# Transformer block on one core: rows dealt 16 to a partition, and gate/up weights loaded by column groups in one ring

## The chip, the cores and the metric

The kernel runs on one core of one Trainium2 chip. Its time is device microseconds of that core, from launch to end. A profile of one execution goes with it: TensorE (PE, and its weight loads PEld), VectorE (DVE), ScalarE (ACT), GpSimd (POOL), SyncE (SP) and the 16 DMA engines.

## The reference

The input x has 2048 tokens (rows) of 448 features, in bf16. Part A is a linear attention block with 16 heads of 28, part B a gated MLP of width 1792. Every step works on one row alone except the two sums over all tokens (kv and z).

```python
n = layernorm(x)
q, k, v = split(n @ wqkv)                      # 16 heads of 28
pq, pk = phi(q), phi(k)                        # phi(t) = (t + 1 if t > 0 else exp(t)) + 1e-6
kv = sum over tokens of pk (x) v ;  z = sum over tokens of pk
o = (pq @ kv) / (pq . z + 1e-6)
h = x + o @ wo
m = layernorm(h)
out = h + (gelu_tanh(m @ w_gate) * (m @ w_up)) @ w_down
```

## The kernel before, in words

The 2048 rows are 16 tiles of 128. `xv` and `outv` (the views of x and the output in DRAM) deal row t*128 + p to partition p of tile t. All x stays in `x_sb`, and the results are written into it before they go out.

*Order of the work.* The kernel is a list of numbered tasks with their buffers. For each engine the string `ORDERS` gives the order in which its queue holds them; semaphores carry the dependences between engines. An engine never overtakes: what stands behind a waiting instruction waits too. The task numbers shift when a task is added, so the strings of two versions can't be compared number by number. SP's queue issues nearly all DMAs, ACT's queue a few.

*Stage 1, attention sums.* For each tile, DVE takes layer-norm statistics (L347, L348), ACT makes the reciprocal deviation (L354, L356), DVE (tiles 0 to 3, L369) or POOL (the others, L351 and L387) normalizes into `xnn`, a ring of six tiles. The normalized tile is transposed into `xnT`: tiles 0 to 3 on PE (L377) with evictions on ACT and DVE, the others by a DMA transpose that SP issues (L389). Then the K projection (L403 with `wk_sb`, 4 matmuls), its feature map on ACT and DVE (L414 to L416), and `pt`, the sum over tokens of normalized x times pk (L422, 4 matmuls, accumulated over all tiles in four PSUM banks). Q projections (L403 with `wq_sb`) are put between them and behind them.

*Stage 2, turn to outputs.* After the last `pt`, its sums are evicted, kv is made with `wv_sb` (L459), masked on DVE (L463), multiplied with `wo_sb` (L468) and evicted to `w2` (L471, L473). For each pair of tiles, function `a2_pair`: the query features (L480, L481), their products with z (`t1`, L485, nearly all on POOL), a reduction to the denominators `den` (L488), the added epsilon (L490), the reciprocal (L491), and the scaled features `pqn` (L492). These are transposed to `pqnT`: pair 0 on PE (L501), the others by DMA (L507). PE multiplies with `w2` (L520), DVE adds x (L526), and a second layer norm gives `hn` (L538, L555), which is transposed to `hnT` (tiles 0 and 1 on PE at L547, the others by DMA at L558).

*Stage 3, MLP.* In chunks of 2, 2, 4, 4 and 4 tiles, `gu_chunk` multiplies with gate and up. The 448 features lie in seven pieces of 64: gate's weights occupy partitions 0 to 63 of `wgu_sb`, up's partitions 64 to 127, and a gate matmul (L600) runs beside an up matmul (L602). ACT applies gelu (L620), DVE multiplies (L622), `b2_tile` does the down projection (L572), the last add (L576) and the store (L577). The work of later pairs is interleaved with the chunks.

*Loads.* Helper `dma` (its issue is L281) keeps the loads of one queue in order. `dma_w3` loads the first 384 rows of a weight, `dma_w1` the last 64, which wait for POOL's zero fill of their padding (L299). SP's queue before: x tile 0, wk, x 2–3, wq, x 4–5, x 6–7, x 8–11, x 12–15, wv, three token transposes, wv's tail, nine token transposes, wo, gate, then pair 1's `pqnT` transpose, w_down, and so on. ACT's queue: x tile 1, the tails of wk and wq, and, behind the landing of the last token transpose, up. Gate and up are one DMA each, 1568 KB.

Of the kernel before, what the change touches and what calls it, by code (L numbers as in the profile page):

```python
# [6 lines left out]
F32 = mybir.dt.float32  # L7
# [7 lines left out]
ORDERS = (  # L15
    "29 35 37 66 46 44 76 71 62 64 53 55 79 92 82 70 87 75 131 86 102 114 91 126 106 141 118 153 130 165 145 177"
    " 157 169 194 189 204 181 216 228 193 243 208 220 232 247 248 233 258 252 287 249 289 293 291 255 264 295 311"
    " 261 313 315 267 316 276 270 273 352 329 333 430 435 440 445 450 455 383 460 502 414 465 507 512 517 522 527"
    " 468 532 574 579 584 486 537 589 594 599 604 609 614 619 624 629 634 639 558 540 671 647 702 644 653 718 723"
    " 728 733 650 738 743 748 753 758 763 768 773 778 783 800 805 810 815 820 825 830 835 840 845 850 855 860 865"  # L20
    " 788 791 794 797 870 873 876 879 882",
    "4 6 9 28 32 33 41 36 42 59 60 45 50 51 67 78 77 54 97 72 98 109 63 93 110 83 80 121 122 94 88 136 81 137 148"
    " 149 133 160 132 103 172 115 173 161 127 142 184 211 199 223 185 212 200 224 154 238 166 239 178 195 190 205"
    " 196 217 229 244 280 281 284 234 285 260 254 253 259 235 250 290 251 294 256 266 312 257 314 263 265 269 268"
    " 262 323 277 324 272 325 326 271 278 275 330 274 335 433 431 438 436 443 441 448 446 453 451 456 458 461 463"
    " 503 505 508 510 515 513 518 520 525 523 528 530 535 533 575 577 582 580 585 587 590 592 597 595 600 602 605"
    " 607 612 610 615 617 620 622 625 627 630 632 640 635 637 642 721 719 726 724 731 734 736 729 741 739 744 746"
    " 751 749 756 754 759 761 766 764 769 771 774 776 781 779 786 784 801 803 806 808 811 813 816 818 823 821 826"
    " 828 833 831 838 836 841 843 848 846 851 853 858 856 863 861 868 866",
    "30 31 39 34 40 57 38 58 43 48 61 49 47 107 52 95 65 96 68 56 108 69 73 119 74 134 120 146 135 84 158 85 159"  # L30
    " 147 89 170 90 171 221 182 104 105 116 197 117 338 198 128 209 222 210 183 129 236 143 299 144 237 155 297 156"
    " 167 168 179 298 180 191 300 336 192 206 368 207 218 219 230 339 231 337 369 245 246 283 282 301 286 303 370"
    " 307 304 308 305 309 288 342 306 343 346 292 310 347 401 344 296 348 345 349 317 399 318 371 319 320 374 321"
    " 327 322 375 328 378 331 376 332 402 353 334 356 400 354 357 355 358 377 434 432 379 409 380 439 437 410 405"
    " 381 444 442 687 471 411 363 449 406 447 543 689 545 473 407 366 408 472 412 452 454 459 546 457 387 384 388"
    " 474 389 690 544 477 385 386 504 464 418 481 462 415 419 506 420 416 417 394 478 482 397 509 511 553 656 483"
    " 516 554 514 425 519 658 521 428 466 657 659 479 484 480 526 531 524 549 688 529 555 536 534 666 576 550 578"
    " 556 581 662 583 588 551 490 552 667 469 491 487 586 591 593 663 664 598 596 488 489 601 603 668 693 492 606"
    " 608 613 694 611 616 500 618 695 621 623 697 626 628 669 698 631 633 699 497 665 696 641 700 538 636 559 562"
    " 563 541 564 560 561 643 672 675 676 569 648 673 677 572 674 706 638 703 645 704 722 720 705 727 682 725 732"  # L40
    " 707 708 654 730 737 735 716 713 742 740 745 747 752 750 757 755 760 762 685 767 765 770 772 775 777 651 782"
    " 780 787 785 802 804 807 809 812 814 817 819 824 822 827 829 834 832 839 837 842 844 849 847 852 854 859 857"
    " 862 867 864 789 792 869 795 798 871 874 877 880 883",
    "17 0 1 18 19 20 22 21 23 26 24 99 111 100 27 112 2 123 124 138 162 150 139 174 151 163 175 186 213 225 201 187"
    " 240 202 25 214 226 241 302 340 341 372 373 404 403 360 359 361 365 362 475 476 547 391 390 392 393 396 548 421"
    " 422 423 424 427 660 661 692 691 493 494 495 496 499 566 565 567 568 571 679 678 680 681 684 710 711 709 715"
    " 712",
    "3 5 7 8 10 11 12 13 14 101 113 125 15 140 152 164 176 188 203 215 227 242 16 279 350 351 382 364 367 413 395"
    " 398 426 467 429 485 557 470 498 670 501 701 539 542 573 570 655 717 646 683 714 649 686 652 790 796 793 799"
    " 875 872 881 878 884",  # L50
)
# [119 lines left out]
def bass_sequential_preLN__linear_attn_block__glu_gated_geglu__prompt_kernel(  # L171
# [4 lines left out]
    NG, GW = 4, 112  # L176
    NK = 7
    NJ = FF // 128
    EPS_LN, EPS = 1e-5, 1e-6
# [9 lines left out]
    with es:  # L189
        block = es.enter_context(nc.Block())  # L190

        def sb(name, shape, dt):
            return es.enter_context(nc.sbuf_tensor(name, shape, dt))
# [36 lines left out]
        t1 = sb("t1", [128, 2, D], F32)  # L230
        den = sb("den", [128, 4, H], F32)
        rd = sb("rd", [128, 4, H], F32)
# [17 lines left out]
        b_wk, b_wq, b_wv = bufs("wk", 2), bufs("wq", 2), bufs("wv", 2)  # L250
        b_wo, b_wg, b_wu, b_wd = _Buf("wo"), _Buf("wg"), _Buf("wu"), _Buf("wd")
        b_ident, b_ones, b_mones, b_mtmp, b_mask, b_eps, b_mhalf, b_powtmp = (
# [21 lines left out]

        xv = A_x[0].rearrange("(t p) d -> p t d", p=128)
        outv = out[0].rearrange("(t p) d -> p t d", p=128)

# [7 lines left out]
        def op(eng, fn, r, w, name, after=()):  # L285
            return G.add(eng, fn, r=r, w=w, name=name, after=after)

        def dma_w3(q, dst, c0, b, name):
            return dma(q, dst[:, 0:3, :], A_wqkv[0:384, c0:c0 + D].rearrange("(k p) n -> p k n", p=128), [b[0]], name)

        def dma_w1(q, dst, c0, b, name):
            return dma(q, dst[A_, 3, :], A_wqkv[384:448, c0:c0 + D], [b[1]], name)


        def dma_x(q, a, b):
            dma(q, x_sb[:, a:b, :], xv[:, a:b, :], b_x[a:b], "dx%d" % a)
# [5 lines left out]
        dma_w3("sp", wk_sb, D, b_wk, "dwk")  # L302
        tk = dma_w1("act", wk_sb, D, b_wk, "dwk_t")
        dma_x("sp", 2, 4)
        dma_w3("sp", wq_sb, 0, b_wq, "dwq")
        dma_w1("act", wq_sb, 0, b_wq, "dwq_t")
        dma_x("sp", 4, 6)
        dma_x("sp", 6, 8)
        dma_x("sp", 8, 12)
        dma_x("sp", 12, 16)  # L310
        dma_w3("sp", wv_sb, 2 * D, b_wv, "dwv")
        dma_w1("sp", wv_sb, 2 * D, b_wv, "dwv_t")
        dma("sp", wo_sb[:, :, :], A_wo.rearrange("(g p) n -> p g n", p=GW), [b_wo], "dwo")

# [49 lines left out]
        def ln_tile(t):  # L364
# [20 lines left out]
            else:  # L385
                ln_negm(t, t + 1, mv1, nm1, b_mv1, b_nm1, "1")
                op("pool", lambda e: e.tensor_scalar(xnn[:, i, 0:D], x_sb[:, t, :], nm1[:, t:t + 1], rs1[:, t:t + 1], ALU.add, ALU.mult),  # L387
                   [b_x[t], b_nm1[t], b_rs1[t]], [b_xn[i]], "normP_%d" % t)
                G.add("sp", lambda e: e.dma_start_transpose(xnT[:, t, :, :], xnn[:, i, :]), r=[b_xn[i], b_ones2], w=b_xnT[t], name="xT_%d" % t, kind="dma")  # L389

# [50 lines left out]
        xts = [t for t in G.all if t.name.startswith("xT_")]  # L441
        dma("sp", wgu_sb[A_, :, :], B_w_gate.rearrange("(k p) n -> p k n", p=64), [b_wg], "dwg", after=xts[-1:])
        dma("act", wgu_sb[B_, :, :], B_w_up.rearrange("(k p) n -> p k n", p=64), [b_wu], "dwu", r=b_xnT[T - 1])

# [31 lines left out]
        def a2_pair(p):  # L476
# [9 lines left out]
            for t in (a, a + 1):  # L486
                n, i = t % 2, t % 4
                op("dve", lambda e, n=n, i=i: e.tensor_reduce(den[:, i, :], t1[:, n, :].rearrange("p (h d) -> p h d", h=H), AX.X, ALU.add),  # L488
                   [b_t1[n]], [b_den[i]], "dr_%d" % t)
                op("dve", lambda e, i=i: e.tensor_scalar(den[:, i, :], den[:, i, :], EPS, None, ALU.add), [b_den[i]], [b_den[i]], "de_%d" % t)  # L490
                op("dve", lambda e, i=i: e.reciprocal(rd[:, i, :], den[:, i, :]), [b_den[i]], [b_rd[i]], "rd_%d" % t)  # L491
                op("dve", lambda e, t=t, n=n, i=i, i2=i2: e.tensor_tensor(  # L492
                    pqn[:, i2, n, :, 0:GW].rearrange("p g (h d) -> p g h d", h=4), pq[:, t, :].rearrange("p (g h d) -> p g h d", g=NG, h=4),
                    rd[:, i, :].rearrange("p (g h) -> p g h", g=NG).unsqueeze(3).to_broadcast([128, NG, 4, DH]), ALU.mult),
                   [b_pq[t], b_rd[i]], [b_pqn[i2][n]], "pn_%d" % t)
# [85 lines left out]
        def gu_chunk(t0, nt):  # L581
# [4 lines left out]
            for j0 in range(0, NJ, nj):  # L586
# [5 lines left out]
                def fngu(e, W, j0=j0, psG=psG, psU=psU):  # L592
# [10 lines left out]
                    return ins  # L603
                G.add("pe", fngu, r=[b_hnT[t % HR] for t in tiles] + [b_wg, (b_wu, 1)], w=[(b_ps[BK_G[i]], 0), (b_ps[BK_U[i]], 1)], name="gu%d_%d" % (nt, v), mw=True)
                for hh_ in range(2):
# [82 lines left out]
```

## Time and profile before

| | us |
|---|---|
| median of 5 runs | 200.31 (198.77 to 202.58) |
| profiled execution, own time | 202.58 |
| its span, first to last instruction | 200.8 |
| PE busy | 191.4 (95%), 1572 matmuls |
| DVE busy | 133.2 (66%) |
| ACT busy | 74.4 (37%) |
| POOL busy | 50.4 (25%) |
| mean granted TensorE clock | 0.983 |
| gate load, issue to landing | 14.6 |
| up load, issue to landing | 17.1 |

The profile cuts the span into 40 slices of 5 us; a digit is the busy share of an engine in a slice in tenths (9 is 90% or more), and PEclk is the clock that the TensorE was granted, in tenths. In the timeline, a line gives the start, the duration, the engine, the source line, the operation, what it writes and reads, and in brackets how long the engine was idle before it and what the profile holds responsible; "SPq" and "ACTq" are DMA issues. Ends of matmuls are modelled, so distances between starts tell PE's pace better than durations. The profiled execution is the slowest of the five runs.

### The profile page before, as it was taken

How to read it: one execution, taken by the hardware profiler on the slowest of the kernel's cores; microseconds unless marked ns; L12 is line 12 of the kernel's file. 1: busy time of each engine (PE TensorE's matmuls, PEld its weight loads, DVE VectorE, ACT ScalarE, POOL GpSimd, SP SyncE). 2: the span in 40 equal slices, each digit the busy share in tenths (PEclk: the TensorE clock that was granted, in tenths of full speed). 3: DMA queues.
4: the chain of work that ended last, by engine and by line, in shares of the span. 5: the costliest groups of instructions: out<-in, count | busy, mean ns of one | idle time of the engine just before them, and what ended most of it. 6: DMA issues, size and time to landing. Idle time of an engine off the chain costs nothing.

```text
span 200.8 us, 4146 instructions
## 1 busy us (share of the span) xinstructions
PE 191.4 (95%) x1572; PEld 109.7 (55%) x1572; DVE 133.2 (66%) x371; ACT 74.4 (37%) x210; POOL 50.4 (25%) x92
## 2 busy tenths in 40 slices
PE   7899999988699989999999999999999999999993
PEld 7454455544478657854444355544455667745563
DVE  2899859899478988968686889536455554433221
ACT  3796543888533221413043220022334434410000
POOL 6074640632270278144004005505000000000000
PEclk9999999999759999999999999999999999999999
DMA  5945448999902912570300092400802000000211
GB/s 171 361 114 83 92 86 207 210 217 137 344 3 42 134 25 45 121 98 0 75 3 0 12 172 64 91 0 26 175 23 56 0 0 3 0 11 16 69 46 49
DMA packets 36180, 16.98 MB, mean 85 GB/s; under 512 B 27712, under 2 KB 35264, under 8 KB 36160
## 3 DMA queue, kind: packets, MB, share of 16 engines
q1 hardware_dynamic: 35392, 14.88, 34.9%
q10 hardware_dynamic: 768, 1.84, 4.3%
q8 instruction: 12, 0.20, 0.4%
q14 instruction: 8, 0.07, 0.1%
HBM read 8.26 MB, written 1.84 MB: 50 GB/s over the span
## 4 chain that ended last, share of the span: by engine, by line
PE 74%; DVE 15%; DMA 6%; SPq 1%; issue 1%; ACT 0%; POOL 0%; ACTq 0%; DVEq 0%
PE ps L600 28%; PE ps L572 21%; PE ps L602 11%; PE ps L520 5%; PE ps L403 4%; PE ps L422 4%; DVE st L347 2%; DMA hnT<-hn 2%; DMA x_sb<-in_A_x_dram 2%; DVE den L488 2%; DMA xnT<-xnn 1%; DVE pqn L492 1%; DVE hh L622 1%; DVE den L490 1%; SPq L281 1%
## 5 line engine op out<-in xcount | busy, mean ns | idle before, releaser
L600 PE MATMUL ps<-hnT,wgu_sb 64*128 64x512 bf16 (+1 forms) x490 | 88.8, 340 | 1.4 <-DVE hnT L553 0.7
L602 PE MATMUL ps<-hnT,wgu_sb 64*128 64x512 bf16 (+1 forms) x490 | 89.4, 340 | 0.1
L620 ACT ACTIVATE gl<-ps 128x256 bf16<-128x256 f32 x112 | 36.9, 381 | 83.7 <-PE ps L602 79.5
L622 DVE TENSOR_TENSOR hh<-ps,gl 128x256 bf16<-128x256 f32 x112 | 43.4, 419 | 35.4 <-ACT gl L620 35.2
L600 PEld LDWEIGHTS ps<-hnT,wgu_sb 64*128 64x128 bf16 x490 | 45.9, 96 | 24.8 <-issue 2.2
L602 PEld LDWEIGHTS ps<-hnT,wgu_sb 64*128 64x128 bf16 x490 | 43.6, 96 | 11.7 <-DVE hh L622 5.2
L572 PE MATMUL ps<-wd_sb,hh 128*128 128x448 bf16 (+1 forms) x238 | 43.8, 342 | 0.0
L572 PEld LDWEIGHTS ps<-wd_sb,hh 128*128 128x128 bf16 x238 | 23.0, 98 | 19.9 <-issue 1.1
L485 POOL TENSOR_TENSOR t<-pq,zbc 128x448 f32<-128x448 bf16 x15 | 17.1, 1146 | 40.2 <-DVE pq L481 20.9
L347 DVE BATCH_NORM_STATS2 st<-x_sb 128x6 f32<-128x448 bf16 x32 | 19.5, 616 | 3.9 <-DMA x_sb<-in_A_x_dram 3.9
L576 DVE TENSOR_TENSOR x_sb<-ps,x_sb 128x448 bf16<-128x448 f32 (+1 forms) x17 | 10.1, 594 | 16.4 <-PE ps L572 16.4
L520 PE MATMUL ps<-w,pqnT 112*128 112x448 bf16 x64 | 13.7, 353 | 1.8 <-DVE pq L481 1.8
L403 PE MATMUL ps<-wk_sb,xnT 128*128 128x448 bf16 x64 | 14.4, 352 | 0.9 <-ACT rs L356 0.5
L422 PE MATMUL ps<-pk,xnn 128*128 128x448 bf16 x64 | 14.1, 352 | 0.0
L403 PE MATMUL ps<-wq_sb,xnT 128*128 128x448 bf16 x64 | 13.8, 352 | 0.0
L526 DVE TENSOR_TENSOR x_sb<-ps,x_sb 128x448 bf16<-128x448 f32 x16 | 9.6, 616 | 2.5 <-PE ps L520 2.5
L414 ACT ACTIVATE e<-ps 128x448 bf16<-128x448 f32 x16 | 8.7, 544 | 6.6 <-PE ps L403 5.8
L555 POOL TENSOR_SCALAR hn<-x_sb,nm,rs 128x448 bf16<-128x448 bf16 x14 | 10.2, 734 | 0.8 <-POOL rs L360 0.2
L520 PEld LDWEIGHTS ps<-w,pqnT 112*128 112x128 bf16 x64 | 5.8, 97 | 8.3 <-DVE pq L481 2.2
L403 PEld LDWEIGHTS ps<-wk_sb,xnT 128*128 128x128 bf16 x64 | 5.9, 97 | 7.6 <-ACT e L414 0.9
L387 POOL TENSOR_SCALAR xnn<-x_sb,nm,rs 128x448 bf16<-128x448 bf16 x12 | 8.7, 726 | 5.2 <-PE ps L422 1.6
L416 DVE SCALAR_TENSOR_TENSOR pk<-ps,e 128x448 bf16<-128x448 f32 x16 | 9.8, 614 | 0.1
(67 smaller groups left out, 139.7 us busy)
## 6 DMA issues: line engine op xcount, KB each, us to landing
out_dram<-x_sb SPq DMA_DIRECT2D x15, 112.0 KB, 1.8
wgu_sb<-in_B_w_gate_dram SPq DMA_DIRECT2D x1, 1568.0 KB, 14.6
wgu_sb<-in_B_w_up_dram ACTq DMA_DIRECT2D x1, 1568.0 KB, 17.1
wd_sb<-in_B_w_down_dram SPq DMA_DIRECT2D x1, 1568.0 KB, 8.0
x_sb<-in_A_x_dram SPq DMA_DIRECT2D x2, 448.0 KB, 5.9
x_sb<-in_A_x_dram SPq DMA_DIRECT2D x3, 224.0 KB, 4.6
wo_sb<-in_A_wo_dram SPq DMA_DIRECT2D x1, 392.0 KB, 3.8
wk_sb<-in_A_wqkv_dram SPq DMA_DIRECT2D x1, 336.0 KB, 3.7
```

The costliest lines, as they stand in the source:

```text
L347: op("dve", lambda e: e.bn_stats(st[:, t, :], src_ap), [b_src], [b_st[t]], "bnst%s_%d" % (tag, t))
L403: ins = e.matmul(ps[:, bk, 0:D], xnT[:, t, k, :], w[:, k, :], start=(k == 0), stop=(k == 3))
L422: ins = e.matmul(ps[:, BK_PT[c], 0:D], xnn[:, t % XN_R, c * 128:(c + 1) * 128], pk[:, i, :], start=(t == 0), stop=(t == T - 1))
L485: op(eng, lambda e, t=t, n=n: e.tensor_tensor(t1[:, n, :], pq[:, t, :], zbc[:, :], ALU.mult), [b_pq[t]] + b_z, [b_t1[n]], "t1%s_%d" % (eng ...
L520: ins = e.matmul(ps[:, BK_OUT[n], 0:D], pqnT[0:GW, i2, n, g, :], w2[:, g, :], start=(g == 0), stop=(g == NG - 1))
L555: op("pool", lambda e, t=t, sh=sh: e.tensor_scalar(hn[:, sh, 0:D], x_sb[:, t, :], nm2[:, t:t + 1], rs2[:, t:t + 1], ALU.add, ALU.mult), [b ...
L572: ins = e.matmul(psO, hh[:, j, (t % HR) * 128:(t % HR + 1) * 128], wd_sb[:, j, c0:c1], start=(j == 0), stop=(j == NJ - 1))
L576: op("dve", lambda e, t=t, psO=psO, c0=c0, c1=c1: e.tensor_tensor(x_sb[:, t, c0:c1], psO, x_sb[:, t, c0:c1], ALU.add), [b_ps[bk], b_x[t]], ...
L600: e.matmul(psG[:, jj * N:(jj + 1) * N], wgu_sb[A_, k, j * 128:(j + 1) * 128], hnT[A_, ka_, c0:c0 + N], start=(k == 0), stop=(k == NK - 1))
L602: ins = e.matmul(psU[:, jj * N:(jj + 1) * N], wgu_sb[B_, k, j * 128:(j + 1) * 128], hnT[B_, kb_, c0:c0 + N], start=(k == 0), stop=(k == NK ...
L620: G.add("act", lambda e, gi=gi, cs_=cs_, psG=psG: e.activation(gl[:, gi, cs_], psG[:, cs_], AF.Gelu_apprx_tanh), r=[b_ps[BK_G[i]]], w=[b_g ...
L622: op("dve", lambda e, dst=dst, srcU=srcU, srcL=srcL: e.tensor_tensor(dst, srcU, srcL, ALU.mult), [b_ps[BK_U[i]], b_glh], [b_ar[j_][t % HR] ...
```

## The change

- `xv` and `outv` deal row p*16 + t to partition p of tile t, so that a partition holds 16 neighbouring rows. Which rows make a tile changes, nothing else; a load of several tiles now reads one contiguous piece for each partition, and a store of one tile writes rows 16 apart.
- The x loads are 0, 1, 2–3, 4–7, 8–11, 12–15 instead of having 4–5 and 6–7 apart. wq and its tail go out ahead of tiles 2–3, all on SP's queue.
- All token transposes stand behind the last load of stage 1 (wo) on SP's queue: wv's tail and wo no longer stand between or behind them.
- Gate and up are split by columns (768 and 1024 of 1792), in the order gate, up, gate, up, all on SP's queue behind the last token transpose. The gate/up matmuls wait for the column group that they read.
- `den` gets a trailing axis of two, of which element 0 is used: it is read and written with a step of two.
- The five engine orders are new. On PE: K0, Q0, K1, Q1 now stand ahead of the transposes of tiles 2 and 3; in stage 2, 8 Q matmuls stand ahead of all four w2 matmuls, 8 behind them, and pair 0's 8 output matmuls follow each other; in stage 3, the outputs of pair 3 stand behind 84 gate/up matmul instructions (with what is left of the first chunk) instead of 56, and the later down projections are grouped differently. On POOL, the zero fill of wk moves behind four other fills.

```diff
-        den = sb("den", [128, 4, H], F32)
+        den = sb("den", [128, 4, H, 2], F32)
...
-        xv = A_x[0].rearrange("(t p) d -> p t d", p=128)
-        outv = out[0].rearrange("(t p) d -> p t d", p=128)
+        xv = A_x[0].rearrange("(p t) d -> p t d", t=T)
+        outv = out[0].rearrange("(p t) d -> p t d", t=T)
...
         tk = dma_w1("act", wk_sb, D, b_wk, "dwk_t")
+        dma_w3("sp", wq_sb, 0, b_wq, "dwq")
+        dma_w1("sp", wq_sb, 0, b_wq, "dwq_t")
         dma_x("sp", 2, 4)
-        dma_w3("sp", wq_sb, 0, b_wq, "dwq")
-        dma_w1("act", wq_sb, 0, b_wq, "dwq_t")
-        dma_x("sp", 4, 6)
-        dma_x("sp", 6, 8)
+        dma_x("sp", 4, 8)
...
-        dma("sp", wo_sb[:, :, :], A_wo.rearrange("(g p) n -> p g n", p=GW), [b_wo], "dwo")
+        two = dma("sp", wo_sb[:, :, :], A_wo.rearrange("(g p) n -> p g n", p=GW), [b_wo], "dwo")
...
-                G.add("sp", lambda e: e.dma_start_transpose(xnT[:, t, :, :], xnn[:, i, :]), r=[b_xn[i], b_ones2], w=b_xnT[t], name="xT_%d" % t, kind="dma")
+                G.add("sp", lambda e: e.dma_start_transpose(xnT[:, t, :, :], xnn[:, i, :]), r=[b_xn[i], b_ones2], w=b_xnT[t], name="xT_%d" % t, kind="dma", after=[two])
...
-        dma("sp", wgu_sb[A_, :, :], B_w_gate.rearrange("(k p) n -> p k n", p=64), [b_wg], "dwg", after=xts[-1:])
-        dma("act", wgu_sb[B_, :, :], B_w_up.rearrange("(k p) n -> p k n", p=64), [b_wu], "dwu", r=b_xnT[T - 1])
+        for i in range(2):
+            cs = slice(0, FC) if i == 0 else slice(FC, FF)
+            dma("sp", wgu_sb[A_, :, cs], B_w_gate[:, cs].rearrange("(k p) n -> p k n", p=64), [b_wg[i]], "dwg%d" % i, after=xts[-1:])
+            dma("sp", wgu_sb[B_, :, cs], B_w_up[:, cs].rearrange("(k p) n -> p k n", p=64), [b_wu[i]], "dwu%d" % i, after=xts[-1:])
...
-                op("dve", lambda e, i=i: e.tensor_scalar(den[:, i, :], den[:, i, :], EPS, None, ALU.add), [b_den[i]], [b_den[i]], "de_%d" % t)
+                op("dve", lambda e, i=i: e.tensor_scalar(den[:, i, :, 0], den[:, i, :, 0], EPS, None, ALU.add), [b_den[i]], [b_den[i]], "de_%d" % t)
```

`FC` is 768. The reduction that writes `den` and the reciprocal that reads it use the same strided view. The strings of `ORDERS` are replaced as a whole and not shown.

## The prediction

> **What bounds the kernel now.** I read the busy slices first. TensorE is busy 95% of the 200.8 us span, so the question is only where it is not, or where it runs slowly.
>
> ```profile
> PE   7899999988699989999999999999999999999993
> PEclk9999999999759999999999999999999999999999
> DMA  5945448999902912570300092400802000000211
> GB/s 171 361 114 83 92 86 207 210 217 137 344 3 42 134 25 45 121 98 0 75 3 0 12 172 64 91 0 26 175 23 56 0 0 3 0 11 16 69 46 49
> ```
>
> Each slice is 5 us. Three things stand out: the first slices; PE digits 8 and 6 in 45–55 us, with the clock falling (7, 5) in 50–60 us; and DMA near full at only 207–217 GB/s in 30–45 us, where the x loads at 5–10 us had 361. The stage windows put numbers on the second:
>
> ```profile
> 50.00:55.00 5.00, 3.21 (x22) 2.24 (x22) 2.30 (x7) 2.69 (x7) 1.03 (x1) 0.79 1.04 347
> 55.00:60.00 5.00, 4.71 (x48) 3.44 (x50) 3.94 (x12) 2.16 (x4) 3.40 (x6) 0.53 0.01 3
> ```
>
> The columns are the five engines' busy times, granted clock, DMA share, GB/s: PE idles 1.8 us, then runs at half clock. The timeline tells what it waited for:
>
> ```profile
> 15.70 1.45 SPq L281 DMA_DIRECT2D wv_sb<-in_A_wqkv_dram  x1
> 18.19 0.93 PE L403 MATMUL ps<-wk_sb,xnT 128*128 128x448 bf16 x4 [0.21 <-DMA xnT<-xnn]
> 20.03 0.92 PE L403 MATMUL ps<-wk_sb,xnT 128*128 128x448 bf16 x4 [0.15 <-DMA xnT<-xnn]
> ...
> 29.97 0.58 SPq L281 DMA_DIRECT2D wo_sb<-in_A_wo_dram  x1
> 30.59 0.65 SPq L281 DMA_DIRECT2D wgu_sb<-in_B_w_gate_dram  x1
> 33.31 0.65 ACTq L281 DMA_DIRECT2D wgu_sb<-in_B_w_up_dram  x1
> ...
> 41.44 1.04 DVE L490 TENSOR_SCALAR den<-den 128x16 f32<-128x16 f32 x1
> ...
> 46.16 1.25 SPq L507 DMA_TRANSPOSE pqnT<-pqn  x1
> 51.37 1.72 PE L520 MATMUL ps<-w,pqnT 112*128 112x448 bf16 x8 [1.82 <-DVE pq L481]
> ```
>
> The last line's releaser is misleading: that DVE work was long done. The other operand is pqnT of pair 1, whose transpose was issued at 46.16 and by the trace's landing records landed at 51.23 (5.1 us; the least of its group is 3.0). It was late because the gate and up loads were still running: gate's packets began at 32.7, up's, issued at 33.31 on the other queue, only at 39.7, and the last ended about 49.3. Each 3584-byte packet into 64 partitions took 280 ns; 896 bytes into 128 partitions took 41. So **the wait that sets the start of the MLP (55.29 us) is the end of the gate/up stream**, then 8 output matmuls (1.51), 14 transposes (1.7) and an eviction.
>
> PE's losses against its own steady pace (4 matmuls of 448 columns every 0.76 us), from the distances between starts: 17–22 us 0.81 (xnT transposes late: starts 1.13, 1.07 and 0.89 apart); 39–44 us 1.4 (kvm, then w); 49.5–51.4 2.0; 52.9–55.3 1.7; half clock 2.63 (84 gate/up pairs of 256 columns took 11.59 us, at 0.107 us a pair 8.96); a later hnT wait 0.87 at 70 us.
>
> **Part by part.** The profiled execution took 202.58 us, 1.78 outside the span; that is 2.27 above the median 200.31. I sum against it and subtract the sum from both.
>
> *Start.* The x rows get packets of 1792 and 3584 bytes instead of 896. At 896 they already ran at 358–381 GB/s, so I take no gain. wq now goes ahead of tiles 2 and 3. Before, bytes in this order (1.23 MB) had landed by 6.90; tiles 2–3 alone landed at 5.91: they come 1.0 us later. PE meanwhile has K0, Q0, K1, Q1 (4 x 0.76), now ahead of those transposes, but DVE queues tile 4's statistics (0.62) ahead of the norm of tile 2, and these wait for the load of tiles 4–7, about 8.15. I make Q2 end near 11.2 instead of the equivalent 10.9: **+0.3**, bounds −0.3 and +1.0. The pad of wk moves behind four memsets on POOL, so ACT issues the tail of wk near 2.35 instead of 1.43 and its table load ends 0.25 later, just as the first statistics do (4.11): nothing.
>
> *Token transposes.* wv's tail sat between transposes 6 and 7: 1.53 us of SP (15.66 to 17.19). It and wo now go out first, near 6 us, where SP has been idle until 11.74. The transposes follow each other at 1.31 us as norms allow. PE needs one per 1.5 us (K and its pt), so **−0.81** of waits. Transpose 6, though, was issued before that tail and took 3.75 us instead of 2.45, so part of its lateness has another cause; half the sum stays if this recurs. Net with the start: the attention sums end 0.5 earlier (0 to 1.0).
>
> *Gate/up stream.* Ahead of it go: wo's issue, 0.62; wo's own 0.39 MB, 0.9 us of delay to gate's first packet (issue to first packet is 1.2 where nothing is ahead, here 2.1); the 0.5 from above; the last norm can start up to 0.7 sooner, as pt of tile 8 stands one K group earlier, of which I take none. Start: 32.7 − 2.0 = 30.7. Length: the bytes and the destination halves are unchanged, 448 x 2 packets of 280 ns over 16 engines = 15.7, 16.6 to the slowest engine before. I keep 16.6, so it ends at 47.3 instead of 49.3. The up load leaves ACT's queue (0.65 us, hidden: ACT was waiting for PE there).
>
> Here a rule speaks against the change. The Trainium skill, "DMA: Bandwidth & Descriptors", under Anatomy of one DMA and its bandwidth rule, puts a fixed cost of about 2.0 us on each DMA and advises at least 1 MiB per transfer; four transfers of 0.69 and 0.92 MB for two of 1.6 MB would, by it, cost 2 x 2.0 = +4.0. The rows say otherwise for queued loads: tiles 8–11 and 12–15, 0.46 MB each, landed at 9.53 and 10.75, 376 GB/s, with no room for a fixed cost between. [...]I take 0, and keep +4 as the far end.
>
> *Pair 1.* Its transpose now stands in the same ring behind all four loads. SP can issue it when DVE has pqn of tile 3 (46.12 before; about 45.3 now, with the 0.5 and some reordering), so with the least landing of 3.0 it could land at 48.3; the stream, with the same 1.9 us behind its end as before, says 49.2. PE needs it at about 47.7, so it still waits some 1.5 us. **Out of pair 1 starts at 49.3 instead of 51.37: −2.1.** This includes the 0.5 above and swallows whatever PE gains in 39–47 us: the reordered w2 and Q matmuls and the smaller DVE stalls only lengthen the wait. The 14 transposes, their eviction and the clock drop are kept: PE idles there as long as before. The weight halves for each column group cost nothing: all land before the first gate/up matmul at 53.2, so the split as such buys nothing either.
>
> *den with a stride.* L490 takes 137–180 ns alone, but 530, 1040, 580 and 380 at 39.1, 41.4, 91.5 and 107.0, each beside a POOL instruction reading SBUF: 1.9 us of DVE. If the stride keeps it off the port that POOL uses, those go. The rule: the Trainium skill, "Vector Engine (DVE) Microarchitecture Reference", section 5.1, lets a one-source instruction take both ports when source and destination are in SBUF and the outermost count is even; a step is no bar. 16 fp32 elements at step 2 meet it, so by the rule the stall stays. No row shows a strided case. Bounds: 0 and −0.5 (in 39–47 us covered by pair 1's wait; at 91.5 the stall reaches PE). I take **0**, with the rule. A loss is excluded: same instructions, same counts.
>
> *MLP order.* 84 gate/up matmul instructions (before 56) now stand before the output matmuls of pair 3, and both hn copies of tiles 2–3 close together, so hnT comes sooner: half of the 0.87, **−0.4**, bounds +0.5 and −1.0. Stores keep 896-byte packets, now 14 KB apart in DRAM; only the last (2.25 us from issue to end) is on the path: 0, bounds ±0.2.
>
> Sum: −2.1 − 0.4 = **−2.5**. Own time 202.58 → 200.1; on the median, 200.31 → **197.8**.
>
> **Rivals.**
> - *Clock stays up* (0.20). The drop costs 2.63, and any change in where PE idles may move it. For: it follows a thin window at 50–54 us. Against: that window stays. DVE idles only 1.7 us in 55–70, so at most that much more comes through: 196.1.
> - *Hidden* (0.20). Pair 1's transpose lands no sooner than about 50.9, because transposes stall beside the loads for reasons other than their end (its packets took up to 2.1 us at 48), or the lead is lost again at the hnT wait of 70 us: −0.5, 199.8.
> - *The stride works* (0.10). L490 stays at 0.17 us: 197.3.
> - *The stream grows* (0.06), the slower side. Four smaller transfers, in one ring, with packets of 1536 and 2048 bytes; everything behind waits, pair 1 first. Its lead is 2.0, so it decides from a stream longer than 18.6 us; with the rule's +4.0 the net is +1.5, 201.8; with +5 or more, or the start's +1.0 on top, over 202.3.
> - *Forecast* (0.44): 197.8, its own range 196.6 to 199.2.
>
> **Numbers.** A measurement of this kernel tells about 1% from no change, here 198.3 and 202.3. Faster: about 0.34 of the forecast's 0.44, all of the clock rival, nearly all of the stride's, 0.02 of the hidden: 0.65. Slower: 0.05, from the stream. The range runs from the clock rival with the early norm and the freed DVE added (196.1 − 0.7 − 0.5, and 0.3 for the start) up past the hidden one: 194.6 to 200.4.
>
> **What would show it.** Right: gate's first load issued near 29, transposes of xnT back to back and no PE wait on them at 18–22; pqnT of pair 1 landed near 49; out of pair 1 at 49–50; gate/up starting near 53; L490 still with some instances over 500 ns. Wrong: gate/up starting after 54.5 or before 52; a clock digit of 9 throughout 50–60; L490 uniform at 0.17; PE waits in 6–12 us above 1.5 in sum; DMA digits of 9 lasting more than four slices from 30 us.

## The result, and the profile after

| | before | changed |
|---|---|---|
| median, us | 200.07 (50 runs, 198.50 to 202.58) | 199.07 (29 runs, 198.54 to 199.64) |
| ratio | | 0.9953 (95% interval 0.9939 to 0.9968), that is −0.94 us |
| profiled execution, own time | 202.58 | 198.89 |
| its span | 200.8 | 197.2 |
| mean granted TensorE clock | 0.983 | 1.000 |

The forecast was −2.5 us. The two profiled executions differ by 3.69 us, the medians by 1.0: the one execution of before that had a profile was the slowest of fifty, and that matters for what follows.

The slices of the changed kernel, 4.9 us each:

```profile
PE   7898999999799799989999999999999999999994
PEclk9999999999999999999999999999999999999999
DMA  5976257997907702623200267102630000000112
GB/s 179 358 191 106 60 103 166 222 216 140 316 6 83 121 3 46 128 40 76 57 0 0 32 138 161 39 0 50 140 70 3 0 0 3 0 21 5 47 47 73
```

The clock digits 7 and 5 of before are gone, and so is PE's 6 at 50 to 55 us. The DMA's full slices still run at 216 to 222 GB/s. The two stage windows (busy us and count of PE, PEld, DVE, ACT, POOL, then granted clock, DMA share, GB/s):

```profile
50.00:55.00 5.00, 4.19 (x58) 2.95 (x57) 4.47 (x13) 4.22 (x9) 2.06 (x3) 1.00 0.88 296
55.00:60.00 5.00, 4.64 (x86) 3.90 (x81) 4.69 (x15) 1.84 (x6) 2.82 (x6) 1.00 0.02 4
...
```

PE started 58 matmuls in the first window where it had started 22. In the second it started 86, at a granted clock of 1.00; that number comes up again below. The timeline, with the lines that answer to those of before:

```profile
5.54 0.49 SPq L282 DMA_DIRECT2D wv_sb<-in_A_wqkv_dram  x1
6.08 0.62 SPq L282 DMA_DIRECT2D wo_sb<-in_A_wo_dram  x1
...
16.68 1.67 PE L403 MATMUL ps<-wk_sb,xnT 128*128 128x448 bf16 x8 [0.55 <-DMA xnT<-xnn]
...
29.93 0.66 SPq L282 DMA_DIRECT2D wgu_sb<-in_B_w_gate_dram  x1
30.62 0.63 SPq L282 DMA_DIRECT2D wgu_sb<-in_B_w_up_dram  x1
...
40.91 1.03 DVE L492 TENSOR_SCALAR den<-den 128x16 f32<-128x16 f32 x1
...
46.33 1.25 SPq L509 DMA_TRANSPOSE pqnT<-pqn  x1
49.68 1.67 PE L522 MATMUL ps<-w,pqnT 112*128 112x448 bf16 x8 [0.61 <-DVE mv L348]
```

What the reader is to see: the tail of wv and wo are issued at 5.5 and 6.1 us; there is no wait on xnT at 18 to 22 us any more, but a new one at 16.68, at tile 4 instead of tile 6; pair 1's transpose is issued as late as before (46.33 against 46.16), but its outputs start at 49.68 instead of 51.37 (the releaser named there is misleading again: the transpose landed at 49.55); and the addition of epsilon to the strided den took 1.03 us.

To tell a rule from an accident, the milestones of several executions stand side by side. "MLP" is from the first gate/up matmul to PE's last end, "sums end" is the start of the first PE instruction behind the last `pt`; all from distances between starts and from landing records, in us:

| | sums end | pair 1's transpose issued, landed | first gate/up | MLP | own time |
|---|---|---|---|---|---|
| before, as forecast from | 36.05 | 46.16, 51.23 | 55.29 | 142.37 | 202.58 |
| before again (e1) | 36.67 | 46.77, 50.99 | 54.30 | 140.49 | 199.58 |
| changed | 36.35 | 46.33, 49.55 | 53.13 | 141.08 | 198.89 |
| changed again (e10) | 35.95 | 45.93, 49.15 | 52.72 | 141.13 | 198.50 |
| before with the new loads (e9) | 36.19 | 46.29, 49.53 | 52.84 | 140.37 | 198.03 |
| the same again (e13) | 37.04 | 47.14, 50.36 | 53.68 | 140.35 | 198.80 |
| the same, third (e17) | 36.22 | 46.31, 49.51 | 52.82 | 140.38 | 197.88 |

### The profile page after: what moved, and what is told of

The parts are those of the page before. It is cut to its first block, busy times and chain, and to the rows that moved or that the text cites. A ratio compares the mean times of both kernels' runs of the same rounds, so it can differ in the third digit from the quotient of the medians.

```text
span 197.2 us, 4143 instructions
## 1 busy us (share of the span) xinstructions
PE 187.5 (95%) x1572; PEld 113.2 (57%) x1572; DVE 135.3 (69%) x371; ACT 74.7 (38%) x210; POOL 49.7 (25%) x92
## 4 chain that ended last, share of the span: by engine, by line
PE 75%; DVE 11%; DMA 9%; ACT 1%; POOL 1%; issue 1%; SPq 0%; DVEq 0%; ACTq 0%; POOLq 0%
PE ps L602 24%; PE ps L574 22%; PE ps L604 14%; PE ps L403 6%; PE ps L422 5%; DMA hnT<-hn 4%; PE ps L522 4%; DMA x_sb<-in_A_x_dram 2%; DMA xnT<-xnn 2%; DVE den L490 2%; DVE st L347 1%; DVE den L492 1%; DVE pqn L494 1%; DVE x_sb L528 1%; ACT eq L430 1%
## 5 line engine op out<-in xcount | busy, mean ns | idle before, releaser
L602 PE MATMUL ps<-hnT,wgu_sb 64*128 64x512 bf16 (+1 forms) x490 | 86.4, 333 | 2.7 <-DMA hnT<-hn 2.0
L604 PE MATMUL ps<-hnT,wgu_sb 64*128 64x512 bf16 (+1 forms) x490 | 86.8, 334 | 0.4 <-DVE hh L624 0.4
L624 DVE TENSOR_TENSOR hh<-ps,gl 128x256 bf16<-128x256 f32 x112 | 42.9, 418 | 33.5 <-ACT gl L622 33.2
L602 PEld LDWEIGHTS ps<-hnT,wgu_sb 64*128 64x128 bf16 x490 | 45.1, 94 | 18.5 <-ACT gl L622 2.5
L604 PEld LDWEIGHTS ps<-hnT,wgu_sb 64*128 64x128 bf16 x490 | 42.5, 94 | 12.2 <-DVE hh L624 6.5
L487 POOL TENSOR_TENSOR t<-pq,zbc 128x448 f32<-128x448 bf16 x15 | 16.2, 1087 | 38.8 <-DVE pq L483 25.3
L347 DVE BATCH_NORM_STATS2 st<-x_sb 128x6 f32<-128x448 bf16 x32 | 19.0, 609 | 4.1 <-DMA x_sb<-in_A_x_dram 4.1
```

The costliest lines, as they stand in the source:

```text
L347: op("dve", lambda e: e.bn_stats(st[:, t, :], src_ap), [b_src], [b_st[t]], "bnst%s_%d" % (tag, t))
L487: op(eng, lambda e, t=t, n=n: e.tensor_tensor(t1[:, n, :], pq[:, t, :], zbc[:, :], ALU.mult), [b_pq[t]] + b_z, [b_t1[n]], "t1%s_%d" % (eng ...
L602: e.matmul(psG[:, jj * N:(jj + 1) * N], wgu_sb[A_, k, j * 128:(j + 1) * 128], hnT[A_, ka_, c0:c0 + N], start=(k == 0), stop=(k == NK - 1))
L604: ins = e.matmul(psU[:, jj * N:(jj + 1) * N], wgu_sb[B_, k, j * 128:(j + 1) * 128], hnT[B_, kb_, c0:c0 + N], start=(k == 0), stop=(k == NK ...
L624: op("dve", lambda e, dst=dst, srcU=srcU, srcL=srcL: e.tensor_tensor(dst, srcU, srcL, ALU.mult), [b_ps[BK_U[i]], b_glh], [b_ar[j_][t % HR] ...
```

## The experiments

Ratios are to before, run beside them on the same chip. Theory A at the start was that the traced execution of before was an exception. It was joined by a second one: the loads make a lead, and the new engine orders give a part of it back in the MLP.

**e1: before, unchanged, a second trace.**

> The kernel before, unchanged, for a second trace of it. Theory A (the profiled execution of before was an exceptional one, so that the sum took a gain from a stall and a clock drop that most executions do not have): its own time is near 200 us, gate/up starts near 54.3 or earlier instead of 55.29, the second pair's pqnT transpose lands within 3.5 us of its issue, and the first 84 gate/up pairs take near 10 us. Theory B (the stall is the rule, and the changed kernel gives its lead back at the hnT transposes): gate/up again starts near 55.3 and the hnT waits of before cost some 1 us less than those of the changed kernel (1.57 against 2.76 us). Ratio to itself 1.000 within 0.2% for both.

Measured: ratio 0.9988 (0.9967 to 1.0009). Its slices:

```profile
PE   7998999979699899999999999999999999999993
PEclk9999999999999999999999999999999999999999
```

And its timeline at the turn to the MLP:

```profile
46.77 1.25 SPq L507 DMA_TRANSPOSE pqnT<-pqn  x1
...
51.12 1.67 PE L520 MATMUL ps<-w,pqnT 112*128 112x448 bf16 x8 [0.96 <-DVE den L488]
...
54.30 0.28 PE L600 MATMUL ps<-hnT,wgu_sb 64*128 64x256 bf16 x1 [0.72 <-DVE hnT L553]
```

Both theories hold in part. The clock never drops here: between the outputs of pair 1 and gate/up there are 3.18 us instead of 3.92, and the first 84 gate/up pairs take 9.66 us instead of 11.59. That part was the exception. The late transpose is the rule: 4.2 us from issue to landing, just behind the landing of up at 50.13, if by less than the 5.1 of the forecast's trace. And e1's hnT waits (0.74 us for tiles 2 and 3) are smaller than those of the changed kernel (1.25), as theory B had it in sign.

**e2, e3, e4: rows and den's stride by themselves.**

```diff
e2 (on before)
-        xv = A_x[0].rearrange("(t p) d -> p t d", p=128)
+        xv = A_x[0].rearrange("(p t) d -> p t d", t=T)      # outv likewise
e3 (on the changed kernel): the same lines back
e4 (on the changed kernel)
-        den = sb("den", [128, 4, H, 2], F32)
+        den = sb("den", [128, 4, H], F32)
```

> Before with the tokens dealt in the new way (two lines: the views of x and out), all else as before. Theory A (row dealing is idle: loads and stores are off the path): ratio 1.000 within 0.2%. Rival (larger pieces make the x tiles land sooner and the stores cheaper, and most of the measured 0.94 us is theirs): 0.995 to 0.997, with x tiles 8 to 15 landing at least 0.5 us sooner and the last store landing sooner after its issue.

> The changed kernel with the old dealing of tokens (row t*128+p), all else as changed. Theory A (row dealing is idle): ratio to before 0.995, as the changed kernel itself. Rival (the dealing carries the gain): 0.998 to 1.001.

> The changed kernel with den packed again (stride 1), all else as changed. Theory A (the stride avoids nothing: the addition of eps still took 1.03 us beside POOL's t1 in the changed kernel): ratio to before 0.995, and the eps additions of the second half show one or two of over 0.5 us, as with the stride. Rival (the stride shortened most of them): 0.997 to 1.000, with at least three of them over 0.5 us.

Measured: e2 1.0025 (1.0003 to 1.0047), e3 0.9983 (0.9963 to 1.0003), e4 0.9969 (0.9951 to 0.9987). By e2 row dealing costs half a microsecond, by e3 taking it away costs about as much (0.9983 against 0.9953); the two speak against each other and are both near the edge of what such runs tell. On the whole the dealing is worth some 0.3% at most, and its sign is not settled. The rival's mechanism did not show: in e2 the last x tiles landed at 11.40 us, in e1 at 10.95, and the last store took 2.08 us from issue to landing, in e1 2.13. For den one line of each kernel decides, the durations (least, median, most) of the epsilon additions. Changed kernel, with the stride:

```profile
L492 DVE TENSOR_SCALAR den<-den x16: 113/170/1035, 38.8 to 104.7; 128x16 f32<-128x16 f32 x16
```

e4, without:

```profile
L492 DVE TENSOR_SCALAR den<-den x16: 110/165/1035, 39.1 to 105.1; 128x16 f32<-128x16 f32 x16
```

Nearly the same three numbers, and in both kernels three of the sixteen took over 0.5 us: the step of two did not shorten the long ones.

**e5, e6: the loads alone, first try.** Before, with the loads moved and nothing else.

```diff
SP's order (15 is wv's tail, 16 wo, 279 gate, 280 up, 101 the first token transpose)
-    "3 5 7 8 10 11 12 13 14 101 113 125 15 140 ... 242 16 279 350 ..."
+    "3 5 7 8 10 11 12 13 14 15 16 101 113 125 140 ... 242 279 350 ..."
e6 besides
-        dma("act", wgu_sb[B_, :, :], ..., [b_wu], "dwu", r=b_xnT[T - 1])
+        dma("sp", wgu_sb[B_, :, :], ..., [b_wu], "dwu", after=xts[-1:])
```

> Before with one part of the change alone: the loads of wv's tail and wo are issued ahead of the token transposes instead of between and behind them; up stays on ACT's ring, one load each for gate and up, before's orders on the other engines. Theory A (wo's 392 KB out of the gate/up stream is the part that brings the lead): the stream ends near 48.7 instead of 50.1, the second pair's pqnT transpose lands near 49.9 instead of 51.0, gate/up starts near 53.3; and because before's order on VectorE stays, none of it is given back: ratio 0.992 to 0.995. Rival (the lead needs the whole of it, the stream still holds the transpose up): gate/up at 54 or later, ratio 0.998 to 1.000. For both: one of the first three token transposes still takes 4 us or more from issue to landing, since its stall goes with the 16 KB instruction fetch near 14 to 16 us and not with wv's tail.

> As e5, and up's load besides on SyncE's ring right behind gate's (still one load each). What is left of the difference to the changed kernel is then the split by columns, the dealing of rows, den's stride and the orders of the engines. Theory A (the orders of the changed kernel give back 0.6 us in the MLP, and the split buys nothing): ratio 0.991 to 0.994, below the changed kernel's 0.995. Rival (the split and the new orders carry the gain): 0.996 to 1.000.

Measured: 1.0083 (1.0051 to 1.0114) and 1.0084 (1.0055 to 1.0113), both slower. e5's waits on SP tell why:

```profile
SPq L281 <- POOL nm L351: 7.3, 1, 7.3
```

SP stood 7.3 us at wv's tail. That load writes beside the padding that POOL clears, and before's POOL order clears it late. All token transposes stood behind it: the first was issued at 14.31, and PE waited 2.63 us for it in one piece. The granted clock fell as well (0.991 over the profiled execution of each; under 0.993 in 16 of their 23 runs), so the loss is not that wait alone. Both expectations fail on a step that I had not followed: moving a load past a queue of transposes moves its wait there too. The changed kernel avoids this in its POOL order, which clears wv's padding ahead of the token norms; the forecast had not followed that step. The pair tells nothing on the stream.

**e9, e13, e17: the loads alone, second try.** e6 with POOL's clearing (task 2) moved forward.

```diff
-    "17 0 1 18 19 20 22 21 23 26 24 99 111 100 27 112 2 123 ..."
+    "17 0 1 18 19 20 22 21 23 26 2 24 99 111 100 27 112 123 ..."
```

> e6 without its flaw: in e5 and e6 SyncE stood from 6 to 13 us, ahead of the token transposes, at wv's tail, which has to wait for the memset of its padding, and POOL does that late in before's order. Here the memset goes where the changed kernel has it on POOL. The kernel is then before with the loads of the changed one but for the split by columns. Theory A (loads make the whole lead, new orders and split give back or nothing): wo lands near 13.6, the first token transpose is issued near 12.3, gate/up starts near 53.2, and the MLP takes what it takes in before: ratio 0.990 to 0.994. Rival (new orders and split are needed for the lead): gate/up after 53.8 or ratio 0.996 to 1.000.

> e9 once more, beside the two that follow, since it had seven runs only. Ratio to before 0.988 to 0.993; if it comes out over 0.995, the reading that the new orders give back half of the lead falls.

> e9 a third time (before with the loads of the change but for the split), beside e16 on the same chip, to set the distance between the two with more runs: ratio 0.989 to 0.994; a distance under 0.1% to e16 would say that the new orders give nothing back.

Measured: 0.9902 (0.9864 to 0.9939), 0.9937 (0.9907 to 0.9967), 0.9913 (0.9881 to 0.9946). Over the three, 21 runs with a median of 198.48, against 199.07 for the 46 runs of the changed kernel (with e10); side by side on one chip 198.03 against 199.06 (e9 and e10), and 198.49 against 199.39 for e16, which is nearly the changed kernel. **Four edits around the loads make the whole lead and more; the changed kernel has 0.6 us less of it.** The windows of e9 show it at the place:

```profile
50.00:55.00 5.00, 4.28 (x62) 3.29 (x61) 4.84 (x14) 4.74 (x10) 2.09 (x3) 1.00 0.87 292
55.00:60.00 5.00, 5.00 (x89) 4.04 (x87) 5.00 (x18) 2.09 (x7) 2.80 (x5) 1.00 0.02 5
...
```

PE is busy all of 55 to 60 us, DVE too; the changed kernel leaves 0.36 us of it idle on PE. In the table above, e9, e13 and e17 need 140.35 to 140.38 us for the MLP, the changed kernel 141.08 and 141.13 (e3 141.10, e4 141.20).

**e7, e11: what in the new orders costs it.** In the changed kernel DVE does this around the norms of tiles 2 and 3 (statistics, aggregates, and the wraps L559, copies that the hnT transposes read), with the transposes' issue and the waits on PE for tiles 2 and 3 and for tiles 4 to 7:

```profile
54.34 1.15 DVE L347 BATCH_NORM_STATS2 st<-x_sb 128x6 f32<-128x448 bf16 x2
55.95 0.17 DVE L348 BATCH_NORM_AGGREGATE mv<-st 128x2 f32<-128x6 f32 x1
57.65 0.17 DVE L348 BATCH_NORM_AGGREGATE mv<-st 128x2 f32<-128x6 f32 x1
61.47 0.26 DVE L559 COPY hn<-hn 128x448 bf16<-128x448 bf16 x1
61.76 3.19 SPq L560 DMA_TRANSPOSE hnT<-hn  x2
61.83 0.27 DVE L559 COPY hn<-hn 128x448 bf16<-128x448 bf16 x1
67.60 0.27 PE L602 MATMUL ps<-hnT,wgu_sb 64*128 64x256 bf16 x1 [1.04 <-DMA hnT<-hn]
...
86.66 0.37 PE L602 MATMUL ps<-hnT,wgu_sb 64*128 64x512 bf16 x1 [0.98 <-DMA hnT<-hn]
```

The second aggregate comes 1.7 us behind the first, for two hh products (gelu times up), a reciprocal, a pqn and another hh stand between. In e1 both were one group, and the transposes were issued at 61.45 although gate/up had started 1.2 us later:

```profile
56.05 0.30 DVE L348 BATCH_NORM_AGGREGATE mv<-st 128x2 f32<-128x6 f32 x2
61.19 0.20 DVE L557 COPY hn<-hn 128x448 bf16<-128x448 bf16 x1
61.45 3.00 SPq L558 DMA_TRANSPOSE hnT<-hn  x2
```

e7 moves the aggregate (task 356) back, e11 the two wraps (364, 367) as well:

```diff
e7
-    " ... 380 359 435 433 381 378 438 356 440 382 445 443"
+    " ... 380 359 356 435 433 381 378 438 440 382 445 443"
e11 besides
-    " 544 406 448 407 450 364 474 367 410 ..."
+    " 364 544 367 406 448 407 450 474 410 ..."
```

> The changed kernel with one VectorE instruction moved: the 0.17 us aggregate of tile 2's second layer norm goes right behind that of tile 3, ahead of the first two hh evictions, a reciprocal, a pqn and another hh, as it stood in before. Theory A (this order is what gives the lead back): POOL's rstd starts near 56.3 instead of 57.9, the hnT transposes of tiles 2 and 3 are issued near 60.2 and 61.5 instead of 61.8 and 63.0, the wait of 1.25 us at gate/up of the second pair falls under 0.5, ratio 0.990 to 0.993. Rival (an instruction fetch near 62.6 us holds the transposes until 65.5 whenever they are issued): the wait stays over 1 us, ratio 0.994 to 0.996.

> The changed kernel once more, as the measure for the three others of this call: ratio 0.994 to 0.997, hT transposes of tiles 2 and 3 held up by the fetch near 62.6 us as in its first trace.

> e7 with two more VectorE instructions moved. In e7 the norms of tiles 2 and 3 ended 1.7 us sooner (59.5 us), but the two wraps (0.27 us copies on VectorE, which the hnT transposes read) stayed at 61.4 and 61.7, behind three hh evictions and a reduce. Here they follow the third pair of hh. Theory A (VectorE's order gives the lead back): hT of tiles 2 and 3 are issued near 60.1 and 61.4, landed by 65.5 even where the fetch near 62.6 hits both, the wait at gate/up of the second pair falls from 1.25 to under 0.6: ratio to before 0.991 to 0.994. Rival (the fetch decides): landed after 66.5 all the same, ratio as the changed kernel's.

Measured: e7 0.9977 (0.9955 to 0.9999), no gain; e10 0.9960 (0.9934 to 0.9987); e11 0.9899 (0.9864 to 0.9934), median 198.43 against e10's 199.06. e7's expectation missed the wraps: POOL's norms did end 1.7 us sooner, but the transposes were issued at 61.67 all the same. With the wraps moved they go out at 60.02:

```profile
55.68 0.23 DVE L348 BATCH_NORM_AGGREGATE mv<-st 128x2 f32<-128x6 f32 x2
59.43 0.27 DVE L559 COPY hn<-hn 128x448 bf16<-128x448 bf16 x1
59.80 0.27 DVE L559 COPY hn<-hn 128x448 bf16<-128x448 bf16 x1
60.02 2.60 SPq L560 DMA_TRANSPOSE hnT<-hn  x2
...
86.00 0.37 PE L602 MATMUL ps<-hnT,wgu_sb 64*128 64x512 bf16 x1 [1.45 <-DMA hnT<-hn]
```

At the first gate/up of tiles 2 and 3 PE no longer waits (0.2 us a little later), and MLP falls from 141.13 to 140.71, although the wait for tiles 4 to 7 grows from 1.25 to 1.72 us (by distances between starts; e1 and e9 have none there). So three DVE instructions in the wrong place hold some 0.4 of the 0.7 us. The rest is a balance of two losses and a gain: the first 84 pairs still take 10.18 us (10.11 in the changed kernel, 9.66 in e1), the wait for tiles 4 to 7 stands, and behind that wait the new order is the faster one, by 1.15 us against e9. What makes these three was not taken apart further.

**e8, e12, e15: what stalls a DMA transpose.** Besides the load rings the trace holds a queue 8, marked "instruction": twelve packets of 16 KB, the first at 14.34 us in the changed kernel. The Trainium skill, "Runtime: NRT & Kernel Launch", section "Instruction fetch mechanics", has each engine refill its instruction memory in blocks of 16 KiB, 256 instructions, and calls the cost mostly hidden. The trace agrees with the block: from the sixth fetch on they come 228 to 276 TensorE instructions apart. From the DMA transposes they are not hidden. If these fetches belong to TensorE, 14 more warm-up matmuls (28 instructions, with the weight loads) must move each of them.

```diff
e8 (on the changed kernel)
-    WARM = 40
+    WARM = 54
e12 (on e11) and e15 (on e9): WARM = 54, and
-                ins = e.matmul(ps[:, 3, 0:128], ones_bf[:], ones_bf[:], start=True, stop=True)
+                ins = e.matmul(ps[:, 3, 0:96], ones_bf[:], ones_bf[:, 0:96], start=True, stop=True)
```

> The changed kernel with 54 warm-up matmuls instead of 40, which fit into TensorE's idle time before the first transposes (start at most 0.15 us later). They move each of the 16 KB instruction fetches on queue 8 earlier by 28 TensorE instructions: the first from 14.3 to near 11.7 us, ahead of the data of the first token transpose. Theory A (the fetch is what holds up the token transposes): the first one lands within 3 us of its issue, the wait of 0.87 us at 14 to 17 us is gone, attention sums end near 35.6. Rival (wv and wo, landing until 13.6 us, hold it up): it lands after 16 us as before and the wait stays. On the total 0 to -0.9 us by theory A, since the later fetches move too and may meet other transposes.

> e11 and 54 warm-up matmuls of 96 columns instead of 40 of 128: the same columns, so no later start than before, but every instruction fetch comes 28 TensorE instructions sooner. In e8 (54 of 128 columns) the warm-up [...]ended 1.2 us too late, and even so the token transposes and hT of tiles 2 and 3 were free of the stall. Theory A (the fetch is what stalls a transpose): the first token transpose lands within 3.2 us, the wait of 0.87 us before K4 is gone, attention sums end near 35.5: ratio 0.986 to 0.990. Rival (no gain from the shift, the fetch only meets others): 0.991 to 0.995.

> e9 with 54 warm-up matmuls of 96 columns instead of 40 of 128, the last run being whether both kernels can be beaten by more. Theory A (the fetch stalls whichever transposes it meets): the first fetch comes near 12.6 instead of 13.75 us, the first token transpose lands within 3.2 us of its issue instead of 4.6, the wait of 0.81 at K4 is gone; against that the fetch near 61.8 still meets hT of tile 2, as in e9. Ratio 0.985 to 0.989. Rival (what is gained at 16 us is lost to another stall later, as in e12 against e11): as e9.

Measured: e8 0.9921 (0.9899 to 0.9943), e12 0.9893 (0.9857 to 0.9928), e15 0.9928 (0.9904 to 0.9951). The fetches did move (e9 to e15: the second from 44.29 to 39.41, the fourth from 62.58 to 61.45; the first less clearly, to between 12.75 and 13.39 us in the three, since without the edit it lay anywhere from 13.65 to 16.76 from trace to trace). The tile views give the time from issue to landing (least, median, most); in the changed kernel first the token transposes, then the hnT transposes of 60 to 70 us:

```profile
DMA to landing us min/median/max: 2.4/2.5/4.3
...
DMA to landing us min/median/max: 3.9/4.2/4.4
```

In e8 the fetch comes at 13.39, 0.2 us behind the first token transpose's issue, and the fourth at 61.34, ahead of the two hnT transposes; the same two lines:

```profile
DMA to landing us min/median/max: 2.4/2.5/3.5
...
DMA to landing us min/median/max: 3.0/3.0/3.0
```

The first three token transposes took at most 2.7 us there, and the wait of 0.87 at K4 (the K projection of tile 4) is gone, as it is in e12 and e15. (The 3.5 in e8 is the seventh, beside an 8 KB packet of queue 14, marked "instruction" too, at 23.8.) Over all 19 traces, 31 token transposes had a fetch of queue 8 begin within 2.4 us behind their issue, and took 3.81 us in the median; the other 197 took 2.48. In the profiled execution of before the fetch came at 15.68, and the transpose issued at 14.39 took 3.75. As a way to gain time it is not reliable. e8's runs gained (median 198.52 against 199.3 for e7 beside it), though its trace, at 199.13 one of its slower runs, doesn't show where. But e12 ends where e11 does, e15 where e13 does. Theory A had the attention sums end near 35.5 us; they ended at 36.30 in e12 and 36.28 in e15, no sooner than in e11 (36.06) and e9 (36.19), and a later fetch meets another transpose (in e15 pair 2's pqnT, 58.67 to 63.48; its MLP took 141.24). In these two that was the rival's expectation, and it was right.

**e14, e16: the split by columns.** e14 is e9 with split, rows and stride and before's orders; e16 is the changed kernel with FC = 1536 instead of 768.

> e9 with the three other parts of the change: gate and up split by columns at 768, tokens dealt in rows of 16, den with stride 2. What is left of the difference to the changed kernel is the orders of the engines (and wq ahead of x tiles 2 and 3, with tiles 4 to 7 in one load). Theory A (these parts do nothing, the orders give back): as e9, 0.988 to 0.993, MLP from first gate/up to last matmul near 140.4 us. Rival (one of these parts costs what the changed kernel lacks): 0.995 to 0.997, MLP near 141.1.

> The changed kernel with the columns of gate and up split at 1536 instead of 768, so that the first load of each brings six sevenths of it. Theory A (the split as such neither gains nor costs, since all pieces land near 48 us and the first gate/up matmul is at 53): ratio to before 0.993 to 0.997, as the changed kernel's, MLP near 141.1 us, pair 1's transpose landed near 49.5. Rival (the split is what the changed kernel loses against e9): 0.988 to 0.992, MLP near 140.5.

Measured: e14 0.9958 (0.9934 to 0.9982), MLP 140.84; e16 0.9945 (0.9927 to 0.9963), MLP 141.61. e16 speaks for theory A: nearly without the split the changed kernel gains nothing towards e9. Its ratio lies 0.32% above that of e17, run beside it; e17's expectation had set 0.1% as the mark, so something is given back. e14 does not settle it by its runs: its ratio is the rival's, but four of its 22 runs had a granted clock of 0.991, the other 18 have a median of 198.68, near e13's 198.62, and e13 has eight runs. Its trace says where its MLP lost: up to the outputs of pair 6 it keeps e9's pace within 0.13 us, and loses 0.49 us there, to one late transpose. These outputs in e9, then in e14, with that transpose's issue:

```profile
115.17 1.68 PE L520 MATMUL ps<-w,pqnT 112*128 112x448 bf16 x8
...
111.06 1.61 SPq L510 DMA_TRANSPOSE pqnT<-pqn  x1
115.74 1.48 PE L523 MATMUL ps<-w,pqnT 112*128 112x448 bf16 x7 [0.32 <-DMA pqnT<-pqn]
```

It took 4.55 us to land, in e9 3.93. The same wait cost 0.54 us in e5, which has none of the three parts, and nothing in e13 and e17. So the MLP shows no steady cost of split, rows and stride. The orders are shown as a cause (e7, e11); that the three parts together cost some tenths of a microsecond is not excluded.

## Why the prediction was wrong, point by point

The time of 199.07 lies in the forecast's own range, because the median of before came out at 200.07; the gain, 0.94 us instead of 2.5, does not fit it. Right was the place: the gate/up stream held pair 1's transpose, and moving the loads freed it. Four smaller loads cost no fixed time each: from gate's first issue to up's last landing 17.8 us (18.1 in e10, 18.4 in e14), against 18.1 in e9, e13 and e17 with two loads in the same ring. So the row that the forecast read (two loads landing 1.22 us apart) was a better guide than the rule of the Trainium skill, "DMA: Bandwidth & Descriptors"; its fit was taken of DMAs that GpSimd issues, and these go out from SP. The stride did nothing, as the prediction had read it out of "Vector Engine (DVE) Microarchitecture Reference", section 5.1.

Met by luck were two times on the way. The stream's last packet ended at 47.22 (forecast 47.3), but it began at 31.37 instead of 30.7 and was 15.85 us long instead of 16.6. Pair 1's transpose landed at 49.55 (forecast 49.2), but not because of the stream's end: in the changed kernel, and in 15 other traces, it landed 3.2 to 3.3 us after its issue, with the stream's last packet ending 0.8 to 1.8 us behind that issue. Only where the stream ended 2.6 us (e2), 2.8 us (e1) or 3.4 us (before) behind it did the landing take 4.1, 4.2 and 5.1 us. So in the changed kernel the issue at 46.33 decides, which waits for DVE's pqn of tile 3. The forecast had it at 45.3, from attention sums that would end sooner; they did not. A still shorter stream could win no more than 0.2 us here (the least landing is 3.0).

Wrong were these terms:

1. *The start of gate/up, −2.1.* The number 53.2 was met (53.13), by two errors that cancel: the outputs of pair 1 start 0.38 later than forecast (49.68), and from there to gate/up it takes 3.45 us instead of the 3.92 that the forecast kept, clock drop and all. In before's second trace (e1) there is no drop, and gate/up starts at 54.30. So the lead is 1.17 us: the outputs of pair 1 start 1.44 sooner (51.12 to 49.68; 0.44 of it an earlier issue of the transpose, 1.00 its shorter landing), and from there to gate/up the changed kernel loses 0.27 (3.18 to 3.45). The step that failed is taking one profiled execution, 2.27 above its median, as the measure of a stall and then subtracting the result from the median.
2. *Token transposes, −0.81.* The wait did not go, it moved from tiles 6 to 8 to tile 4 (0.87). The forecast had seen the sign, a transpose issued ahead of wv's tail that took 3.75 us, and gave it half the sum; by e8 the cause is an instruction fetch that meets transposes in flight, not the tail. "Attention sums 0.5 earlier" came to 0.3 earlier against e1 and to 0.3 later against the other trace of before.
3. *MLP order, −0.4.* The sign was wrong. Against e1 it measured +0.59 (140.49 to 141.08): the first 84 pairs +0.46, the wait for tiles 2 and 3 +0.51, from there to the first matmul of tiles 4 to 7 +0.90 (a wait of 1.25 us for their hnT, which e1 does not have), and everything behind that −1.28, with fewer changes between gate/up and other matmuls. "Both hn copies close together, so hnT comes sooner" looked at two instructions and not at what stands before them on DVE: the aggregate behind a row of products. In before's order e9 has 140.37.
4. *"Nothing" for wk's padding.* ACT issued wk's tail at 2.29 instead of 1.43, and it landed at 6.96 instead of 5.26; K0's last matmul waited 0.24 us for it. The start as a whole came out as forecast: Q2 ended at 11.29 (11.2), and TensorE's losses in 6 to 12 us came to 0.92, under the 1.5 allowed.

The sum against e1: −1.17 + 0.59, and 0.11 less behind the last matmul, is −0.69; the medians give −0.94. Of the rivals, the clock's came true in the trace and was worth nothing on the median, because it had nothing to remove there; "hidden" foresaw a lead lost again at the hnT wait, and its −0.5 is nearer to −0.94 than the forecast's −2.5, though pair 1's transpose did land early.

## What to carry to other kernels

Before a stall in one profiled execution is booked as a gain, see where that execution stands among its runs: a second trace of the same kernel would have taken 0.99 us out of this sum (gate/up at 54.30 instead of 55.29). A lead at the start of a stage is kept only if the next chain that feeds it moves up too, so follow that chain on every engine to its last copy (here an aggregate and two wraps), and when a load is moved ahead, follow what it waits for. Where a new order and a new load scheme come together, try the loads with the old order.

## What the runs showed of the hardware

An instruction fetch of 16 KB, 0.9 to 1.6 us long, held up DMA transposes in flight: a token tile took 3.81 us in the median instead of 2.48, an hnT tile 4.37 (50 of them) instead of 2.96 (216). From the fourth fetch on its place follows the count of TensorE instructions, so 28 more of them at the start shift which transpose is hit through the rest of the kernel. Pair 1's transpose, issued while the weight stream ran, landed 3.2 to 3.3 us after its issue when the stream ended at most 1.8 us behind that issue (16 traces), and 4.1 to 5.1 us after it when the stream ended 2.6 to 3.4 us behind it (3 traces). The clock drop that took 2.6 us in the profiled execution of before is rare: of the 178 runs of before beside e1, e5, e10 and e14, eight had a granted clock under 0.993, and these took 201.3 to 203.3 us; of the changed kernel's 46 none had.
